# Four changes to a forward-and-backward kernel of linear and windowed attention: grouped score products, TensorE transposes, larger DMAs, an overlapped linear backward

## The chip, the cores and the metric

The kernel runs on one core of a Trainium2 chip. The metric is the device time of one execution in microseconds (us), the median of several runs. The runs of one kernel in one call lay within 0.1 to 0.7% of each other, and the changed kernel run a second time, on another occasion, was 0.4% away from the first by its ratio and 0.6% in microseconds (below). So differences of whole runs under about 20 us are not trusted here; differences inside one stage of the trace, which repeat better, are.

## The reference

The input is a sequence of 2048 rows of 640 values. Four layers follow each other: linear attention (A), windowed attention (B), A, B, with shared weights, a layer norm ahead of each and a residual around each. There are 32 heads of 20 values. The outputs are the result of the forward pass and the gradients of the input and of the four weight matrices.

```python
def A(x, wqkv, wo):                       # linear attention
    q, k, v = split(x @ wqkv)             # 32 heads of 20
    phi = lambda t: where(t > 0, t + 1, exp(t)) + 1e-6
    kv = einsum("sd,se->de", phi(k), v);  z = phi(k).sum(0)
    return (phi(q) @ kv / (phi(q) @ z + 1e-6)) @ wo

def B(x, wqkv, wo):                       # window of 256
    q, k, v = split(x @ wqkv)
    s = where(0 <= i - j < 256, q @ k.T / sqrt(20), -1e9)
    return (softmax(s) @ v) @ wo

for L in (A, B, A, B): x = x + L(layernorm(x))
# outputs: x, and the gradients of sum(x * grad_out)
```

## The kernel before

The kernel goes through the layers in 128-row tiles, in nine stages: the first linear layer; two "forward pairs" (the end of an A layer, a B layer, and the start of the next A layer, interleaved over tiles); then backwards a windowed stage, a linear stage, a windowed stage, the weight gradients of B, a linear stage, and the weight gradients of A. A scheduler orders the instructions of each engine when the program is built; each engine then runs its own list in order. "Priority" below means that the scheduler is told to place these instructions as early as it can.

A windowed backward stage works on 256 steps a layer. A step is one 128-row query tile, two heads, and up to three key tiles. It computes the scores again (`s`), their exponential (`e`, on ScalarE, masked on GpSimd), dP (`dp`), dS = dP * e (`ds`, on VectorE), the transpose of dS (`dsT`), and 18 small products that add up dV, dK and dQ (`acc`). Work on neighbouring tiles (dense products, layer norm gradient) is given out between the steps as filling. The code below is shortened.

```python
# one step: scores now; dP two steps later; the products three steps after that
for j in range(2):
    r0 = HP * (2 * p + j)                      # rows 0,32 or 64,96 of the array
    self.mm(s[:, j, 0:cw], Q["qT"][r0:r0+HP, bi, gs], K["kT"][r0:r0+HP, kk:kk+nb, gs], True, True, (r0, 0))
nc.scalar.activation(e, s, ACT.Exp)            # ... masks on GpSimd
st.q1.append(...); self.core_step(st, l)       # lag1 = 2, lag2 = 3

def core_ds(...):
    dp = st.pD.tile([P, 2, 512], F32)
    for j in range(2):
        self.mm(dp[:, j, 0:cw], Q["dT"][bi][r0:r0+HP, g, :], K["vT"][r0:r0+HP, kk:kk+nb, gs], True, True, (r0, 0))
    nc.vector.tensor_tensor(out=ds, in0=dp, in1=e, op=ALU.mult)
    self.dma(dT, ds, transpose=True)           # one DMA, or two where nb < 3
```

The linear backward is one function that runs a tile from end to end:

```python
def linear_tile(self, st, l, t, WT, g_out):
    # load dn, v, pk, pq of this tile (four DMAs); 18 transposes on TensorE
    # 21 small products -> dqkv (VectorE, ScalarE)
    self.dma(self.rows(self.dq[l], t), dqkv)   # store, 480 KB
    yield from self.tail(st, l, t, dqkv, WT, g_out)
def tail(...):                                 # load hn and g (two DMAs)
    self.dma(dT, dqkv, transpose=True)
    # 30 dense products of dT with WT, then the layer norm gradient, then a store
```

The softmax here doesn't subtract the row's maximum and nothing guards it: scores larger than these inputs give would overflow.

## Time and profile before

The kernel took 3540.01 us (median of 3 runs, 3529.01 to 3542.17).

The first view is the table of busy time by stretch of the kernel before. The stretches are the nine stages in the order named above, cut where the trace shows the first or last instruction of each. The columns are the stretch, its length, the busy time of each engine with its number of instructions (PE is TensorE, PEld its weight loads, DVE VectorE, ACT ScalarE, POOL GpSimd), the mean granted TensorE clock as a share of full speed, the mean busy share of the 16 DMA engines, and what they moved.

```profile
core 0: us, PE busy (x) PEld busy (x) DVE busy (x) ACT busy (x) POOL busy (x), PEclk, DMA share, GB/s
0.00:156.00 156.00, 101.37 (x740) 69.64 (x740) 98.33 (x291) 43.74 (x98) 17.62 (x53) 0.92 0.51 162
156.00:631.00 475.00, 380.07 (x4665) 246.50 (x4665) 265.44 (x676) 210.71 (x218) 166.96 (x274) 0.82 0.48 130
631.00:1008.00 377.00, 291.61 (x4175) 182.10 (x4175) 193.58 (x486) 178.87 (x135) 163.46 (x277) 0.81 0.59 156
1008.00:1793.00 785.00, 584.81 (x6534) 323.67 (x6534) 399.34 (x622) 274.55 (x481) 219.62 (x500) 0.60 0.75 163
1793.00:2088.00 295.00, 138.99 (x1108) 94.74 (x1109) 91.98 (x240) 45.24 (x114) 0.48 (x1) 0.69 0.47 122
2088.00:2862.00 774.00, 580.68 (x6530) 322.23 (x6529) 400.27 (x622) 274.88 (x480) 216.37 (x495) 0.60 0.70 150
2862.00:3051.00 189.00, 175.46 (x960) 94.83 (x960) 10.18 (x17) 6.21 (x13) 0.00 (x0) 0.95 0.56 177
3051.00:3347.00 296.00, 132.18 (x1105) 91.74 (x1104) 92.19 (x241) 44.64 (x112) 0.00 (x0) 0.69 0.62 166
3347.00:3536.00 189.00, 174.98 (x960) 94.56 (x960) 11.29 (x19) 6.18 (x12) 0.00 (x0) 0.96 0.37 121
```

The two windowed stages (785 and 774 us) are 44% of the span, and their TensorE clock is 0.60. The two linear stages (295 and 296 us) have TensorE busy for less than half of the time, and no other engine busier than that: something is waited for one after the other.

The next view is the same table for the scores-to-scores part of the first windowed stage, cut into its first 64 steps (two chunks) and the other 192.

```profile
1032.00:1197.00 165.00, 106.94 (x1150) 54.77 (x1150) 63.54 (x101) 53.83 (x98) 43.26 (x99) 0.53 0.55 127
1197.00:1699.00 502.00, 425.10 (x5029) 238.21 (x5028) 300.65 (x455) 209.50 (x357) 172.91 (x394) 0.61 0.82 170
```

The first 64 steps take 2.6 us each although TensorE is busy in only 65% of the time. What it waits for stands in the view of one tile, dsT, over these steps (the lines say who waited for the tile: microseconds in total, number of times):

```profile
  PEld L142: 62.4, 62
  PE acc L142: 47.7, 50
DMA to landing us min/median/max: 2.2/2.6/5.9
```

(In the second layer the first 64 steps took 183 us, but there the first scores ran ahead, beside the end of the linear stage.)

In the other 192 steps (2.61 us each) TensorE is busy in 85% of the time. How the scores and dP look there is shown by the timeline of TensorE alone (columns: start, length, engine, line, operation and tiles, sizes, number of instructions); both pairs ran at half clock:

```profile
1450.98 0.50 PE L142 MATMUL dp<-vT,dT 32*128 32x384 bf16 x2
...
1451.86 0.50 PE L142 MATMUL s<-kT,qT 32*128 32x384 bf16 x2
1452.29 1.25 PE L142 MATMUL dense<-WoTB,gT 128*128 128x320 bf16 x4
```

The pair of scores started at 1451.86 and the next work at 1452.29: a pair holds the engine for 0.43 us, and a step has two pairs.

In the linear stages the timeline of all engines shows the chain of one tile:

```profile
1912.60 0.32 SPq L117 DMA_DIRECT2D dqkv<-dqa  x1
1912.97 2.82 SPq L117 DMA_TRANSPOSE dqT<-dqa  x1
...
1918.13 5.79 PE L142 MATMUL dense<-WTA,dqT 128*128 128x320 bf16 x30 [8.59 <-DMA dqT<-dqa]
```

The bracket says that TensorE stood idle for 8.59 us until the transpose landed. Over fourteen tiles it waited 124.5 us for this tile, 8.9 us of each 17.2 us:

```profile
  PE dense L142: 124.5, 14
```

### The profile page before, as it was taken

The numbers are of one execution on the slowest core, as the hardware profiler recorded it, in microseconds if no ns is written. First come the engines' busy times: TensorE is split into PE (matmuls) and PEld (weight loads), VectorE is DVE, ScalarE is ACT, GpSimd is POOL, SyncE is SP. The second block draws the span as 40 slices with busy tenths as digits, with TensorE's granted clock in tenths as the row PEclk, the third lists the DMA queues.
The fourth block names the chain that finished last, engine by engine and source line by source line (L and its number), as shares of the span: only waits on it lengthen the run. The fifth ranks groups of instructions, "written<-read, shape, count | busy, mean of one in ns | idle before, by whom it ended". The sixth has DMA issues, their size and how long they took to land. (4 is left out here: it accounts for less than half of the span.)

```text
span 3536.7 us, 66383 instructions
## 1 busy us (share of the span) xinstructions
PE 2560.2 (72%) x26776; PEld 1520.0 (43%) x26776; DVE 1562.6 (44%) x3212; ACT 1085.0 (31%) x1661; POOL 784.5 (22%) x1600
## 2 busy tenths in 40 slices
PE   6787788688855788888544445888888669644499
PEld 4455555355522444444333322444444344333254
DVE  6555555455522566565432332555666410133200
ACT  2244444255532444444111112444444200011100
POOL 1033333245521333333100002333333100000000
PEclk9888788788865565656666665566666689866699
DMA  6455444566564888787654443888886474564542
GB/s 208 116 138 131 128 128 119 151 162 176 150 162 105 161 185 179 174 180 139 166 144 119 120 117 81 173 179 175 175 184 149 118 238 156 141 187 126 163 137 69
DMA packets 964981, 531.60 MB, mean 150 GB/s; under 512 B 686656, under 2 KB 929344, under 8 KB 964672
## 3 DMA queue, kind: packets, MB, share of 16 engines
q1 hardware_dynamic: 964672, 527.35, 60.5%
q8 instruction: 209, 3.42, 0.4%
q14 instruction: 100, 0.82, 0.1%
HBM read 216.53 MB, written 146.54 MB: 103 GB/s over the span
## 5 line engine op out<-in xcount | busy, mean ns | idle before, releaser
L626 DVE TENSOR_TENSOR ds<-dp,e 128x768 bf16<-128x768 f32 (+2 forms) x512 | 463.5, 905 | 375.3 <-PE dp L142 269.7
L595 ACT ACTIVATE e<-s 128x768 bf16<-128x768 f32 (+2 forms) x512 | 394.7, 771 | 495.4 <-PE s L142 270.7
L597 POOL TENSOR_SCALAR_AFFINE_SELECT e<-e 128x256 bf16<-128x256 bf16 x512 | 224.9, 440 | 1224.0 <-ACT e L595 1196.3
L348 ACT ACTIVATE eT<-sT 128x1536 bf16<-128x1536 f32 (+2 forms) x256 | 351.0, 1371 | 368.8 <-PE sT L142 340.3
L142 PEld LDWEIGHTS <-dqT 128*128 128x128 bf16 x1920 | 218.6, 119 | 448.1 <-DMA dqT<-dqa 285.4
L142 PE MATMUL dense<-WTA,dqT 128*128 128x320 bf16 x960 | 190.8, 375 | 281.1 <-DMA dqT<-dqa 281.1
L142 PE MATMUL s<-kT,qT 32*128 32x384 bf16 (+2 forms) x1024 | 267.1, 436 | 91.2 <-ACT e L595 87.1
L142 PE MATMUL acc<-ks,dsT 128*128 128x20 bf16 x2880 | 216.8, 179 | 134.8 <-DMA dsT<-ds 132.9
L142 PE MATMUL acc<-qs,ds 128*128 128x20 bf16 x2880 | 277.3, 179 | 13.4 <-DVE dq L680 11.9
L142 PE MATMUL dp<-vT,dT 32*128 32x384 bf16 (+2 forms) x1024 | 254.4, 441 | 39.1 <-DVE ds L626 34.3
L142 PEld LDWEIGHTS <-ds 128*128 128x128 bf16 x2880 | 212.7, 102 | 133.8 <-issue 128.5
L142 PE MATMUL acc<-ds,e 128*128 128x20 bf16 x2880 | 269.2, 177 | 0.0
L534 ACT ACTIVATE dh<-dense,rs 128x320 f32<-128x320 f32 x128 | 67.5, 527 | 652.9 <-issue 347.9
L350 POOL TENSOR_SCALAR_AFFINE_SELECT eT<-eT 128x512 bf16<-128x512 bf16 x256 | 164.6, 643 | 431.8 <-ACT eT L348 416.4
L142 PE MATMUL wg<-rq,lh 128*128 128x480 bf16 x1280 | 259.5, 366 | 0.0
L142 PEld LDWEIGHTS <-hnT 128*128 128x128 bf16 x1920 | 189.1, 106 | 130.6 <-DVE hnT L184 40.0
L142 PEld LDWEIGHTS <-dsT 128*128 128x128 bf16 x2880 | 155.6, 104 | 205.5 <-DMA dsT<-ds 183.0
L142 PE MATMUL dense<-WTB,dqT 128*128 128x320 bf16 x960 | 197.8, 367 | 29.3 <-DMA dqT<-dqkv 26.8
L142 PEld LDWEIGHTS <-e 128*128 128x128 bf16 x2880 | 211.9, 103 | 15.6 <-issue 9.9
L601 POOL TENSOR_SCALAR_AFFINE_SELECT e<-e 128x256 bf16<-128x256 bf16 x448 | 190.2, 425 | 0.0
L184 DVE COPY dnT<-flip 126x768 bf16<-126x768 bf16 x32 | 17.8, 558 | 380.8 <-PE flip L179 380.8
L142 PE MATMUL dense<-WB,hnT 128*128 128x320 bf16 x960 | 180.0, 334 | 7.0 <-DVE hnT L184 5.9
(132 smaller groups left out, 3800.2 us busy)
## 6 DMA issues: line engine op xcount, KB each, us to landing
rq<-dqkv SPq DMA_DIRECT2D x16, 1920.0 KB, 9.6
qs<-qs SPq DMA_DIRECT2D x64, 256.0 KB, 2.9
qT<-qT SPq DMA_DIRECT2D x64, 256.0 KB, 3.1
dqkv<-dq SPq DMA_DIRECT2D x32, 480.0 KB, 4.4
dqkv<-dqa SPq DMA_DIRECT2D x32, 480.0 KB, 3.4
kT<-kT SPq DMA_DIRECT2D x28, 512.0 KB, 3.9
vT<-vT SPq DMA_DIRECT2D x28, 512.0 KB, 4.1
ks<-ks SPq DMA_DIRECT2D x28, 512.0 KB, 4.4
```

Of the source, the lines that this page charges most:

```text
L142: return self.nc.tensor.matmul(out, lhsT=lhsT, rhs=rhs, start=start, stop=stop, skip_group_check=True, **kw)
L184: eng.tensor_copy(o, t[0:w, 0:n, :])
L348: nc.scalar.activation(e[:, :, 0:nb * P], s[:, :, 0:nb * P], ACT.Exp)
L350: nc.gpsimd.affine_select(out=dg, in_=dg, compare_op=ALU.is_ge, fill=0.0, base=0, pattern=[[0, 4], [1, P]], channel_multiplier=-1)
L534: nc.scalar.activation(dh[:, c * CW:(c + 1) * CW], ps[:, 0:CW], ACT.Copy, scale=rs, accum_out=ac[:, c:c + 1])
L595: nc.scalar.activation(e[:, :, 0:cw], s[:, :, 0:cw], ACT.Exp)
L597: nc.gpsimd.affine_select(out=dg, in_=dg, compare_op=ALU.is_ge, fill=0.0, base=0, pattern=[[0, 2], [-1, P]], channel_multiplier=1)
L601: nc.gpsimd.affine_select(out=fr, in_=fr, compare_op=ALU.is_ge, fill=0.0, base=-1, pattern=[[0, 2], [1, P]], channel_multiplier=-1)
L626: nc.vector.tensor_tensor(out=ds[:, :, 0:cw], in0=dp[:, :, 0:cw], in1=e[:, :, 0:cw], op=ALU.mult)
```

## The change

The change wants to keep TensorE fed in the windowed backward, relieve the DMA queue, and overlap the tiles of the linear backward.

1. **Scores and dP grouped.** Both get priority; dP is issued just ahead of the scores of a later step; the lag goes from 2 to 3, so that the dP pair and the score pair that are issued together are of different p and use opposite halves of the array. The forward scores get priority too.
2. **Half of dS on TensorE.** Steps with p = 1 transpose dS on TensorE and copy it out of PSUM (the memory that TensorE writes to) on VectorE; p = 0 still goes by DMA.
3. **Fewer, larger DMAs.** q, k and v are stored together, q and k transposed in one DMA; per-tile loads of the windowed backward become loads of two tiles, those of the linear backward of four; loads of the next slab are issued at the seventh step of a chunk, not at its start.
4. **Linear backward pipelined.** The tail of tile t-1 (its dense products) is interleaved with tile t, and the transpose is issued before the store.

The diff also gives `e` an eighth buffer, gives the linear backward a third buffer and more of PSUM, and moves one of its copies from VectorE to ScalarE.

```diff
@@ windowed core, per step
+                    if len(st.q1) >= st.lag1:
+                        self.core_dp(st, *st.q1[-st.lag1])
                     s = st.pS.tile([P, 2, 512], F32, name="s")
-                    for j in range(2):
+                    with self.tc.high_priority():
+                        for j in range(2):
                         ... the two score products ...
@@ core_ds
-        dp = ...; the two dP products
+        # moved to core_dp, with priority
         nc.vector.tensor_tensor(out=ds, in0=dp, in1=e, op=ALU.mult)
-        if nb == 3:
+        if p == 1:
+            ps = st.ps.tile([P, 8, P], BF, name="flip", tag="m")
+            for j in range(2):
+                for i in range(nb):
+                    nc.tensor.transpose(ps[:, 3 * j + i, :], ds[:, j, i * P:(i + 1) * P], self.ident)
+            nc.vector.tensor_copy(v(dT), v(ps))
+        elif nb == 3:
             self.dma(dT, ds.rearrange("p j k -> p (j k)"), transpose=True)
-            st.lag1, st.lag2 = 2, 3
+            st.lag1, st.lag2 = 3, 3
@@ backward_linear, N = 4 tiles a load
+                drive(self.linear_tile(st, l, t, L, dT), [(prev, 1.2)] if prev else [])
+                prev = back(t, L, dT)          # the tail of this tile, run beside the next
@@ linear_tile
+        self.dma(dT, dqkv, transpose=True)
         self.dma(self.rows(self.dq[l], t), dqkv)
-        yield from self.tail(st, l, t, dqkv, WT, g_out)
 ... (merged stores and loads cut)
```

More of the change, by code (lines that the diff above doesn't have):

```diff
@@ L90, in __init__ @@
         for l in (0, 2):
-            self.sv[l] = dict(pq=d(f"pq{l}", [T, D]), pk=d(f"pk{l}", [T, D]), v=d(f"v{l}", [T, DA]),
+            self.sv[l] = dict(pqk=d(f"pqk{l}", [T, 2 * D]), v=d(f"v{l}", [T, DA]),
                               dn=d(f"dn{l}", [T, DA]))
         for l in (1, 3):
-            self.sv[l] = {k: d(f"{k}{l}", [TT, P, G * P]) for k in ("qs", "ks", "vs", "qT", "kT", "vT")}
+            self.sv[l] = {k: d(f"{k}{l}", [TT, P, 3, G * P]) for k in ("s", "T")}
         self.ident = const.tile([P, P], BF, name="ident")
@@ L120, in rows, with pair @@
         return ap[t * P:(t + 1) * P, :]
+    def pair(self, ap, c, n=2):
+        return ap[c * n * P:(c + 1) * n * P, :].rearrange("(b p) f -> p b f", p=P)
     def load(self, pool, name, src, shape, dt=BF, bufs=None):
@@ L220, in a_first @@
         sv = self.sv[l]
-        f = {}
+        pqk = st.sb.tile([P, 2, D], BF, name="pqk")
         for j, nm in enumerate(("pk", "v", "pq")):
@@ L226, in a_first @@
             else:
-                pt = st.sb.tile([P, D], BF, name=nm)
+                pt = pqk[:, 0 if nm == "pq" else 1, :]
             for c in range(2):
@@ L241, in a_first @@
                 self.dma(self.rows(sv["v"], t), vt)
-                f["v"] = vt
-                yield from self.acc_outer(st, f["pk"], vt, t == 0)
-            else:
-                self.dma(self.rows(sv[nm], t), pt)
-                f[nm] = pt
+                yield from self.acc_outer(st, pqk[:, 1, :], vt, t == 0)
+        self.dma(self.rows(sv["pqk"], t), pqk.rearrange("p a f -> p (a f)"))
     def acc_outer(self, st, a, b, first):
@@ L275, in a_out @@
         nc = self.nc
-        pq = self.load(st.sb, "pqf", self.rows(self.sv[l]["pq"], t), [P, D])
+        pq = self.load(st.sb, "pqf", self.rows(self.sv[l]["pqk"], t)[:, 0:D], [P, D])
         yield
@@ L315, in b_qkv @@
         R = st.ring[t % len(st.ring)]
-        for j, nm in enumerate(("qs", "ks", "vs")):
-            s = R[nm]
+        for j, nm in enumerate("qkv"):
+            s = R["s"][:, j, :, :]
             for c in range(2):
@@ L320, in b_qkv @@
                 dst = s[:, c * HALF:(c + 1) * HALF, 0:DH]
-                if nm == "qs":
+                if nm == "q":
                     nc.vector.tensor_scalar(out=dst, in0=self.heads(ps[:, 0:CW]), scalar1=CS, scalar2=None, op0=ALU.mult)
@@ L325, in b_qkv @@
                 yield
-            flat = s.rearrange("p h d -> p (h d)")
-            self.dma(sv[nm][t], flat)
-            tn = nm[0] + "T"
-            self.dma(R[tn], flat, transpose=True)
-            self.dma(sv[tn][t], R[tn].rearrange("p g q -> p (g q)"))
-            yield
+            if j == 1:
+                self.dma(R["T"][:, 0:2, :, :].rearrange("p a g q -> p (a g) q"),
+                         R["s"][:, 0:2, :, :].rearrange("p a h d -> p (a h d)"), transpose=True)
+        self.dma(sv["s"][t], R["s"].rearrange("p a h d -> p a (h d)"))
+        self.dma(R["T"][:, 2, :, :], R["s"][:, 2, :, :].rearrange("p h d -> p (h d)"), transpose=True)
+        self.dma(sv["T"][t], R["T"].rearrange("p a g q -> p a (g q)"))
+        yield
     def b_core(self, st, l, t, o):
@@ L338, in b_core @@
         rings = [st.ring[(k0 + i) % len(st.ring)] for i in range(nb)]
-        qT = st.ring[t % len(st.ring)]["qT"]
+        qT = st.ring[t % len(st.ring)]["T"][:, 0, :, :]
         for g in range(G):
             s = st.pS.tile([P, 4, 512], F32, name="sT")
-            for i in range(nb):
-                for hh in range(4):
-                    r0 = HP * hh
-                    self.mm(s[:, hh, i * P:(i + 1) * P], rings[i]["kT"][r0:r0 + HP, g, :], qT[r0:r0 + HP, g, :],
-                            True, True, (r0, 0))
+            with self.tc.high_priority():
+                for i in range(nb):
+                    for hh in range(4):
+                        r0 = HP * hh
+                        self.mm(s[:, hh, i * P:(i + 1) * P], rings[i]["T"][r0:r0 + HP, 1, g, :], qT[r0:r0 + HP, g, :],
+                                True, True, (r0, 0))
             e = st.pe.tile([P, 4, 3 * P], BF, name="eT")
@@ L373, in b_pv @@
                 ins = self.mm(st.ops[:, 4 * q + hh, :], e[:, hh, i * P:(i + 1) * P],
-                              rings[i]["vs"][:, 4 * g + hh, 0:HA], st.first is None, i == nb - 1)
+                              rings[i]["s"][:, 2, 4 * g + hh, 0:HA], st.first is None, i == nb - 1)
                 if st.first is None:
@@ L436, in forward_pair @@
             for i in range(5):
-                R = {}
-                for nm in ("qs", "ks", "vs"):
-                    R[nm] = rp.tile([P, H, HP], BF, name=f"{nm}{i}")
-                    nc.gpsimd.memset(R[nm][:, :, DH:HP], 0.0)
-                    R[nm[0] + "T"] = rp.tile([P, G, P], BF, name=f"{nm[0]}T{i}")
-                nc.gpsimd.memset(R["vs"][:, :, DH:DH + 2], 1.0)
+                R = dict(s=rp.tile([P, 3, H, HP], BF, name=f"s{i}"), T=rp.tile([P, 3, G, P], BF, name=f"T{i}"))
+                nc.gpsimd.memset(R["s"][:, :, :, DH:HP], 0.0)
+                nc.gpsimd.memset(R["s"][:, 2, :, DH:DH + 2], 1.0)
                 st.ring.append(R)
@@ L486, in g_flip_dense, with bd @@
             yield
-    def bd(self, st, l, t, R, WoT):
+    def bd(self, st, l, t, g, o, R, WoT):
         nc = self.nc
-        g = self.load(st.sb, "gb", self.rows(self.gs[l], t), [P, D], bufs=1)
-        o = self.load(st.sb, "ob", self.rows(self.o[l], t), [P, D], bufs=1)
         ds = R["ds"]
         r = self.r[l]
-        yield
         def use(c, ps):
@@ L515, in bd, with tail @@
         yield
-    def tail(self, st, l, t, dqkv, WT, g_out):
+    def tail(self, st, l, t, dT, hn, g, gn, WT):
         nc = self.nc
-        hn = self.load(st.sb, "hnb", self.rows(self.hn[l], t), [P, D])
-        g = self.load(st.sb, "gc", self.rows(self.gs[l], t), [P, D])
-        dT = st.sb.tile([P, NF, P], BF, name="dqT")
-        self.dma(dT, dqkv, transpose=True)
-        yield
         dh = st.sf.tile([P, D], F32, name="dh")
@@ L543, in tail, with a_grad @@
         nc.vector.scalar_tensor_tensor(out=a, in0=hn, scalar=s2, in1=g, op0=ALU.mult, op1=ALU.add)
-        gn = st.sb.tile([P, D], BF, name="gn")
         nc.vector.scalar_tensor_tensor(out=gn, in0=dh, scalar=s1, in1=a, op0=ALU.add, op1=ALU.add)
-        self.dma(self.rows(g_out, t), gn)
-        st.gn = gn
         yield
-    def a_grad(self, st, l, t, g, WoT):
+    def a_grad(self, st, l, t, g, o, pq, dn, WoT):
         nc = self.nc
-        o = self.load(st.sb, "oa", self.rows(self.o[l], t), [P, D], bufs=1)
-        pq = self.load(st.sb, "pqb", self.rows(self.sv[l]["pq"], t), [P, D], bufs=1)
-        dn = st.sb.tile([P, H, HA], BF, name="dn")
         pr = st.sf.tile([P, H, DH], F32, name="prod")
@@ L569, in a_grad @@
         yield
-        flat = dn.rearrange("p h d -> p (h d)")
-        self.dma(self.rows(self.sv[l]["dn"], t), flat)
-        yield from self.acc_outer(st, pq, flat, t == 0)
+        yield from self.acc_outer(st, pq, dn.rearrange("p h d -> p (h d)"), t == 0)
     def core_chunk(self, st, l, c, half, K, Q, dq):
@@ L588, in core_chunk @@
                 for p in range(2):
+                    if len(st.q1) >= st.lag1:
+                        self.core_dp(st, *st.q1[-st.lag1])
                     s = st.pS.tile([P, 2, 512], F32, name="s")
-                    for j in range(2):
-                        r0 = HP * (2 * p + j)
-                        self.mm(s[:, j, 0:cw].rearrange("p (a b) -> p a b", a=nb), Q["qT"][r0:r0 + HP, bi, gs],
-                                K["kT"][r0:r0 + HP, kk:kk + nb, gs], True, True, (r0, 0))
+                    with self.tc.high_priority():
+                        for j in range(2):
+                            r0 = HP * (2 * p + j)
+                            self.mm(s[:, j, 0:cw].rearrange("p (a b) -> p a b", a=nb), Q["qT"][r0:r0 + HP, bi, gs],
+                                    K["kT"][r0:r0 + HP, kk:kk + nb, gs], True, True, (r0, 0))
                     e = st.pe.tile([P, 2, 3 * P], BF, name="e")
@@ L607, in core_step @@
     def core_step(self, st, l, flush=False):
+        if flush and st.q1:
+            self.core_dp(st, *st.q1[0])
         if len(st.q1) > (0 if flush else st.lag1):
@@ L616, in core_flush, with core_dp, v @@
             yield
+    def core_dp(self, st, g, gs, b, bi, p, nb, kk, cw, e, K, Q, dq, c, w0):
+        st.dp = st.pD.tile([P, 2, 512], F32, name="dp")
+        with self.tc.high_priority():
+            for j in range(2):
+                r0 = HP * (2 * p + j)
+                self.mm(st.dp[:, j, 0:cw].rearrange("p (a b) -> p a b", a=nb), Q["dT"][bi][r0:r0 + HP, g, :],
+                        K["vT"][r0:r0 + HP, kk:kk + nb, gs], True, True, (r0, 0))
     def core_ds(self, st, l, g, gs, b, bi, p, nb, kk, cw, e, K, Q, dq, c, w0):
         nc = self.nc
-        dp = st.pD.tile([P, 2, 512], F32, name="dp")
-        for j in range(2):
-            r0 = HP * (2 * p + j)
-            self.mm(dp[:, j, 0:cw].rearrange("p (a b) -> p a b", a=nb), Q["dT"][bi][r0:r0 + HP, g, :],
-                    K["vT"][r0:r0 + HP, kk:kk + nb, gs], True, True, (r0, 0))
         ds = st.pd.tile([P, 2, 3 * P], BF, name="ds")
-        nc.vector.tensor_tensor(out=ds[:, :, 0:cw], in0=dp[:, :, 0:cw], in1=e[:, :, 0:cw], op=ALU.mult)
+        nc.vector.tensor_tensor(out=ds[:, :, 0:cw], in0=st.dp[:, :, 0:cw], in1=e[:, :, 0:cw], op=ALU.mult)
         dT = st.pt.tile([P, 6, P], BF, name="dsT")
-        if nb == 3:
+        if p == 1:
+            ps = st.ps.tile([P, 8, P], BF, name="flip", tag="m")
+            for j in range(2):
+                for i in range(nb):
+                    nc.tensor.transpose(ps[:, 3 * j + i, :], ds[:, j, i * P:(i + 1) * P], self.ident)
+            def v(t):
+                return t[:, 0:6, :].rearrange("p (a b) q -> p a b q", a=2)[:, :, 0:nb, :]
+            nc.vector.tensor_copy(v(dT), v(ps))
+        elif nb == 3:
             self.dma(dT, ds.rearrange("p j k -> p (j k)"), transpose=True)
@@ L702, in backward_window @@
             st.sf = self.pool(es, "sf", 1)
+            st.sp = self.pool(es, "sp", 1)
             st.pS = self.psum(es, "pS", 1)
@@ L705, in backward_window @@
             st.pA = self.psum(es, "pA", 1)
-            st.pe = self.pool(es, "pe", 7)
+            st.pe = self.pool(es, "pe", 8)
             st.pd = self.pool(es, "pd", 5)
             st.pt = self.pool(es, "pt", 4)
-            st.lag1, st.lag2 = 2, 3
+            st.lag1, st.lag2 = 3, 3
             st.q1, st.q2 = [], []
@@ L730, in loads @@
                 Q = {}
-                for nm in ("kT", "vT", "ks"):
+                for nm, k, w in (("kT", "T", 1), ("vT", "T", 2), ("ks", "s", 1)):
                     K[nm] = sl.tile([P, 4, 4 * P], BF, name=nm)
-                    self.dma(K[nm][:, 0:n, :], sv[nm][w0:w0 + n, :, cs].rearrange("t p f -> p t f"))
-                for nm in ("qT", "qs"):
+                    self.dma(K[nm][:, 0:n, :], sv[k][w0:w0 + n, :, w, cs].rearrange("t p f -> p t f"))
+                for nm, k in (("qT", "T"), ("qs", "s")):
                     Q[nm] = sl.tile([P, 2, 4 * P], BF, name=nm)
-                    self.dma(Q[nm], sv[nm][t0:t0 + 2, :, cs].rearrange("t p f -> p t f"))
+                    self.dma(Q[nm], sv[k][t0:t0 + 2, :, 0, cs].rearrange("t p f -> p t f"))
                 for nm in ("ds", "dT"):
@@ L741, in before @@
             def before(c):
+                g = self.load(st.sp, "gb", self.pair(self.gs[l], c), [P, 2, D])
+                o = self.load(st.sp, "ob", self.pair(self.o[l], c), [P, 2, D])
+                yield
+                yield
                 for i in range(2):
                     t = 2 * c + i
-                    yield from self.bd(st, l, t, ring[t % 4], wb["WoT"])
+                    yield from self.bd(st, l, t, g[:, i, :], o[:, i, :], ring[t % 4], wb["WoT"])
             def behind(c):
+                la = l - 1
+                dT = st.sp.tile([P, NF, 2 * P], BF, name="dqT")
+                self.dma(dT, self.dq[l][2 * c * P:(2 * c + 2) * P, :], transpose=True)
+                hn = self.load(st.sp, "hnb", self.pair(self.hn[l], c), [P, 2, D])
+                g = self.load(st.sp, "gc", self.pair(self.gs[l], c), [P, 2, D])
+                yield
+                o = self.load(st.sp, "oa", self.pair(self.o[la], c), [P, 2, D])
+                pq = self.load(st.sp, "pqb", self.pair(self.sv[la]["pqk"], c)[:, :, 0:D], [P, 2, D])
+                gn = st.sp.tile([P, 2, D], BF, name="gn")
+                dn = st.sp.tile([P, 2, H, HA], BF, name="dn")
+                yield
+                yield
+                yield
                 for i in range(2):
                     t = 2 * c + i
-                    yield from self.tail(st, l, t, self.rows(self.dq[l], t), wb["WT"], g_out)
-                    yield from self.a_grad(st, l - 1, t, st.gn, wa["WoT"])
+                    yield from self.tail(st, l, t, dT[:, :, i * P:(i + 1) * P], hn[:, i, :], g[:, i, :], gn[:, i, :], wb["WT"])
+                    if i == 1:
+                        self.dma(self.pair(g_out, c), gn)
+                    yield from self.a_grad(st, la, t, gn[:, i, :], o[:, i, :], pq[:, i, :], dn[:, i, :, :], wa["WoT"])
+                self.dma(self.pair(self.sv[la]["dn"], c), dn.rearrange("p b h d -> p b (h d)"))
             for _ in before(0):
@@ L758, in core @@
                 for half in range(2):
-                    if half == 0:
-                        KQ.append(loads(c, 1))
-                    elif c + 1 < NC:
-                        KQ.append(loads(c + 1, 0))
-                    yield from self.core_chunk(st, l, c, half, *KQ.pop(0), dq)
+                    for i, _ in enumerate(self.core_chunk(st, l, c, half, *KQ.pop(0), dq)):
+                        if i == 6:
+                            if half == 0:
+                                KQ.append(loads(c, 1))
+                            elif c + 1 < NC:
+                                KQ.append(loads(c + 1, 0))
+                        yield
             for c in range(NC):
@@ L780, in backward_linear, with loads, back, linear_tile @@
         sv = self.sv[l]
+        N = 4
         with ExitStack() as es:
-            st = self.state(es, 2, 6)
-            st.sf = self.pool(es, "sf", 2)
-            wa = self.weights(es, "A", ("WT",))
-            for t in range(TT):
-                for _ in self.linear_tile(st, l, t, wa["WT"], g_out):
-                    pass
-    def linear_tile(self, st, l, t, WT, g_out):
+            st = self.state(es, 3, 8)
+            st.sf = self.pool(es, "sf", 3)
+            st.sp = self.pool(es, "sp", 2)
+            WT = self.weights(es, "A", ("WT",))["WT"]
+            def loads(c):
+                L = {}
+                for nm, src, w in (("dn", sv["dn"], DA), ("v", sv["v"], DA), ("pqk", sv["pqk"], 2 * D),
+                                   ("hn", self.hn[l], D), ("g", self.gs[l], D)):
+                    L[nm] = self.load(st.sp, "l" + nm, self.pair(src, c, N), [P, N, w])
+                L["gn"] = st.sp.tile([P, N, D], BF, name="gn4")
+                return L
+            def back(t, L, dT):
+                i = t % N
+                yield from self.tail(st, l, t, dT, L["hn"][:, i, :], L["g"][:, i, :], L["gn"][:, i, :], WT)
+                if i == N - 1:
+                    self.dma(self.pair(g_out, t // N, N), L["gn"])
+            nxt = loads(0)
+            prev = None
+            for t in range(TT):
+                if t % N == 0:
+                    L = nxt
+                if t % N == 2 and t + N < TT + 2:
+                    nxt = loads(t // N + 1)
+                dT = st.sb.tile([P, NF, P], BF, name="dqT")
+                drive(self.linear_tile(st, l, t, L, dT), [(prev, 1.2)] if prev else [])
+                prev = back(t, L, dT)
+            for _ in prev:
+                pass
+    def linear_tile(self, st, l, t, L, dT):
         nc = self.nc
-        sv = self.sv[l]
+        i4 = t % 4
         acols = [HA * h for h in HS]
@@ L794, in linear_tile @@
         dqkv = st.sb.tile([P, QT], BF, name="dqa")
-        src = {}
-        for nm, w in (("dn", DA), ("v", DA), ("pk", D), ("pq", D)):
-            src[nm] = self.load(st.sb, "l" + nm, self.rows(sv[nm], t), [P, w])
+        src = dict(dn=L["dn"][:, i4, :], v=L["v"][:, i4, :], pq=L["pqk"][:, i4, 0:D], pk=L["pqk"][:, i4, D:2 * D])
         fl = {}
-        for nm, K, cols, eng in (("dn", KA, acols, nc.vector), ("v", KA, acols, nc.scalar), ("pk", KB, kcols, nc.vector)):
+        for nm, K, cols, eng in (("dn", KA, acols, nc.vector), ("v", KA, acols, nc.scalar), ("pk", KB, kcols, nc.scalar)):
             fl[nm] = self.flip(st.ps, st.sb, src[nm], nm + "T", K, 6, 0, eng, cols)
@@ L823, in linear_tile @@
                 yield
+        self.dma(dT, dqkv, transpose=True)
         self.dma(self.rows(self.dq[l], t), dqkv)
-        yield from self.tail(st, l, t, dqkv, WT, g_out)
+        yield
     def weight_grads(self, kind, layers):
```

## The prediction

> **What bounds it now.** From first and last instructions, the 3537 us span is: first layer 150 us; forward pairs 495 and 357; windowed backward 783 and 773; linear backward 297 and 295; weight gradients 192 and 190 (untouched). The windowed backward has 512 steps. In its steady chunks (1250 to 1700 us) a step takes 2.63 us; matmul starts in the trace show about 2.08 us of TensorE work and 0.55 us of waits (scores 0.22, dP 0.13, dsT products 0.11). TensorE bounds it, at a clock near 0.62. DMA is close: the table by stretch has it 0.68 to 0.95 busy, over half in 256-byte transpose packets, and SyncE spends 227 of 450 us issuing dsT transposes (1.22 us each). In the first two chunks of a layer (69 steps, 190 us) TensorE works 111 us and waits 56 for dsT. The linear backward is a serial chain: of a 17.2 us tile TensorE waits 8.7 us for the transposed dqa (5.2 us from issue to landing).
>
> **What changes.**
> 1. Lag 3 lets dP and scores use opposite row groups. The Trainium skill (TensorE: Matmul & The Clock Gate, The mechanism) says such matmuls overlap, starting about 4 ns apart; the trace agrees inside a pair, while scores followed by dP on the same rows cost 0.27 us more. But in the built order only about a third of the steps hold all four products together: I expect 0.05 to 0.1 us a step.
> 2. Half of the dsT transposes move to TensorE: 1440 transposes of 0.107 us (clock 0.5) or 0.056 us (1.0), about 0.27 us a step, plus a 0.56 us VectorE copy per two steps (VectorE, 0.6 busy, rises to 0.7). DMA falls from 0.85 to about 0.65 busy. In steady chunks this burdens TensorE, the bound, to relieve DMA, which is not: nearly a wash (2.5 to 2.7 us). In the first two chunks most of the 56 us wait goes. With steadier loads and a paired tail: 50 us a layer.
> 3. Linear backward: the tail of tile t-1 is interleaved with tile t. But in the built order only six transposes stand between tile t's last product and the first dense product that needs its dqT, so the wait stays exposed, about 4.5 us instead of 8.7. A tile takes 13.5 to 15 us; with a slower start: 40 us a stage.
> 4. Forward: scores earlier, fewer DMAs; waits before sT are 22 us in each pair: 10 us a pair.
>
> **Sum.** 3540 - 100 - 80 - 20 = 3340 us; 8 in 10 between 3230 and 3440. Chances: faster by over 2% 0.93, within 2% 0.06, slower 0.01.
>
> **What would show it.** Item 1: starts 4 ns apart across scores and dP in a third of the steps. Item 2: dsT waits in the first chunks mostly gone, a step there about 2.2 us; a steady step near 2.6 us. Item 3: a tile near 14 us, TensorE still waiting 4 to 5 us for dqT. Item 4: pairs 1 to 4% shorter.
>
> **What would make it wrong.** The skill (same page, What's actually happening) has the clock at half or full by recent activity; the trace's clock record agrees (0.5 and 1.0 only). If denser work keeps it at 1.0 longer, steady chunks gain up to 0.4 us a step (150 us). Transposes waiting for VectorE's dS in the in-order queue, or sharing PSUM banks, could cost 0.2 us a step. Bulk loads ahead of dqT could eat item 3.

## The result, and the profile after

The changed kernel took 3312.25 us (median of 3 runs, 3311.65 to 3315.82). The ratio is 0.9367, with a 95% interval of 0.9336 to 0.9399. A ratio here is the mean time of one kernel's runs over that of the kernel before in the same rounds, so it is not quite the ratio of the medians quoted.

The table by stretch of the kernel after, for the same nine stages:

```profile
0.00:151.00 151.00, 98.00 (x744) 68.39 (x745) 98.69 (x291) 43.69 (x98) 17.05 (x43) 0.95 0.50 165
151.00:582.00 431.00, 342.90 (x4666) 232.11 (x4662) 256.07 (x677) 209.61 (x218) 165.49 (x274) 0.89 0.50 144
582.00:979.00 397.00, 292.56 (x4175) 190.64 (x4175) 191.68 (x485) 178.75 (x135) 163.26 (x267) 0.78 0.55 149
979.00:1712.00 733.00, 587.19 (x7261) 365.53 (x7262) 455.80 (x750) 275.23 (x481) 209.90 (x500) 0.67 0.58 138
1712.00:1937.00 225.00, 137.09 (x1099) 101.80 (x1098) 93.54 (x224) 55.56 (x129) 0.00 (x0) 0.74 0.50 142
1937.00:2678.00 741.00, 593.14 (x7254) 366.51 (x7254) 455.27 (x751) 275.41 (x481) 208.99 (x496) 0.67 0.57 134
2678.00:2867.00 189.00, 175.86 (x960) 95.02 (x960) 10.19 (x17) 6.35 (x13) 0.00 (x0) 0.95 0.59 183
2867.00:3108.00 241.00, 138.99 (x1106) 102.95 (x1104) 94.36 (x225) 55.26 (x128) 0.00 (x0) 0.73 0.52 148
3108.00:3309.00 201.00, 174.75 (x960) 94.36 (x960) 10.84 (x18) 6.17 (x12) 0.00 (x0) 0.94 0.56 177
```

Read against the table of before, and with the sums that the prediction made (it cuts the two forward pairs at another place, as 495 and 357 us, where the table above has 475 and 377):

| stages | predicted | measured |
|---|---|---|
| first layer and two forward pairs | -20 | -5, -44, +20: -29 |
| two windowed backward stages | -100 | -52, -33: -85 |
| two linear backward stages | -80 | -70, -55: -125 |
| two weight gradient stages | 0 | 0, +12 |
| sum | -200 | -227 |

The same cut of the first windowed stage into 64 and 192 steps:

```profile
1003.00:1127.00 124.00, 102.28 (x1211) 61.67 (x1211) 72.09 (x126) 52.36 (x96) 44.75 (x102) 0.53 0.52 136
1127.00:1607.00 480.00, 423.32 (x5611) 266.61 (x5612) 341.09 (x542) 211.05 (x357) 162.37 (x392) 0.73 0.60 137
```

The first 64 steps fell from 165 to 124 us, the other 192 from 502 to 480 although TensorE has 12% more instructions to do there; its clock went from 0.61 to 0.73, and the DMA share from 0.82 to 0.60. The waits for dsT in the first 64 steps:

```profile
  PEld L145: 12.8, 15
  PE acc L145: 9.0, 11
DMA to landing us min/median/max: 2.2/2.7/4.5
```

So 47.7 us of waiting before the products became 9.0 us; a single DMA transpose takes as long as before.

The timeline of TensorE shows what a grouped step looks like at half clock:

```profile
1302.88 0.47 PE L145 MATMUL s<-kT,qT 32*128 32x384 bf16 x1 [0.26 <-ACT e L581]
1302.89 0.50 PE L145 MATMUL dp<-vT,dT 32*128 32x384 bf16 x1
1302.89 0.50 PE L145 MATMUL s<-kT,qT 32*128 32x384 bf16 x1
1302.89 0.50 PE L145 MATMUL dp<-vT,dT 32*128 32x384 bf16 x1
1303.32 0.82 PE L623 MATMUL flip<-ident,ds 128*128 128x128 bf16 x6
```

All four products start within about 0.01 us of each other (13 ns in the trace) and hold the engine until 1303.32, for 0.44 us, the time of one pair before. The Trainium skill (TensorE: Matmul & The Clock Gate, The mechanism) has matmuls in different row groups overlap, with starts about 4 ns apart; this trace agrees.

In the linear backward:

```profile
1800.00 4.02 SPq L117 DMA_TRANSPOSE dqT<-dqa  x1
...
1804.08 0.57 SPq L117 DMA_DIRECT2D dqkv<-dqa  x1
...
1806.09 1.51 PE L145 MATMUL dense<-WTA,dqT 128*128 128x320 bf16 x5 [6.59 <-DMA dqT<-dqa]
```

The transpose now goes first and the dense products come in fives between the work of the next tile, but TensorE still stands idle for it, over thirteen tiles 67.5 us, 5.2 us a tile. The tile takes 13.6 us.

```profile
  PE dense L145: 67.5, 13
```

Two stretches got longer. In the second forward pair 377 us became 397. The view of waits there shows what TensorE waited for ahead of the forward scores (sT), the merged transpose of q and k; before the change it waited 3.3 us for the transpose of k:

```profile
PE sT L145 <- DMA T<-s: 20.7, 16, 2.4
```

And between the last scores of a windowed stage and its end, 94 and 93 us became 105 and 102. The longest single wait for DMA there, in the first layer, is for the transposed load of the gradient rows; first the kernel after, then the kernel before:

```profile
engine line waited for: us in total, times, longest us
PEld L145 <- DMA dqT<-dqkv: 14.8, 1, 14.8
PEld L142 <- DMA dqT<-dqkv: 10.3, 1, 10.3
```

In the second layer it went from 9.8 to 11.5 us. The pair of tiles is now loaded into a single buffer, but that is not what held this load: the products that last read the buffer had started by 1599.4 us, and the load was issued at 1632.9 us, when the stores of the rows that it reads (issued at 1628.7 and 1629.3 us) had landed. Most of the loss lies ahead of it: the first of these stores went out 21 and 19 us after the last scores, 14 and 13 us before the change. Why they go out later was not tried.

The last weight gradient stage starts 12 us later because four loads of its right-hand side, which the kernel before had fetched during the linear stage, are issued after that stage; this is read from the timeline and was not tried.

### The profile page after: what moved, and what is told of

Read it like the earlier page. It is cut to its first block, busy times and chain, and to the rows that moved or that the text cites. A ratio compares the mean times of both kernels' runs of the same rounds, so it can differ in the third digit from the quotient of the medians.

```text
span 3309.7 us, 67700 instructions
## 1 busy us (share of the span) xinstructions
PE 2540.5 (77%) x28216; PEld 1617.3 (49%) x28216; DVE 1666.5 (50%) x3436; ACT 1106.0 (33%) x1693; POOL 764.7 (23%) x1580
## 5 line engine op out<-in xcount | busy, mean ns | idle before, releaser
L583 POOL TENSOR_SCALAR_AFFINE_SELECT e<-e 128x256 bf16<-128x256 bf16 x512 | 213.8, 418 | 791.6 <-ACT e L581 774.2
L145 PEld LDWEIGHTS <-dqT 128*128 128x128 bf16 x1920 | 204.1, 118 | 329.1 <-DMA dqT<-dqa 168.2
L145 PE MATMUL dense<-WTA,dqT 128*128 128x320 bf16 x960 | 217.2, 375 | 163.8 <-DMA dqT<-dqa 163.8
L145 PE MATMUL s<-kT,qT 32*128 32x384 bf16 (+2 forms) x1024 | 216.4, 405 | 75.8 <-ACT e L581 67.7
L145 PE MATMUL acc<-qs,ds 128*128 128x20 bf16 x2880 | 264.4, 178 | 9.3 <-DVE dq L679 7.1
L145 PE MATMUL dense<-WTB,dqT 128*128 128x320 bf16 x960 | 210.6, 369 | 40.4 <-DMA dqT<-dqkv 38.0
L145 PE MATMUL dp<-vT,dT 32*128 32x384 bf16 (+2 forms) x1024 | 223.9, 416 | 20.8 <-DVE ds L617 19.2
L898 DVE CAST wr<-wg 128x480 bf16<-128x480 f32 (+1 forms) x36 | 21.7, 602 | 368.2 <-PE wg L145 368.2
L145 PEld LDWEIGHTS <-lh 128*128 128x128 bf16 x1280 | 125.2, 98 | 133.7
L623 PE MATMUL flip<-ident,ds 128*128 128x128 bf16 x1440 | 189.0, 273 | 0.9 <-DVE ds L617 0.9
L587 POOL TENSOR_SCALAR_AFFINE_SELECT e<-e 128x256 bf16<-128x256 bf16 x448 | 183.0, 408 | 0.0
```

The costliest lines, as they stand in the source:

```text
L145: return self.nc.tensor.matmul(out, lhsT=lhsT, rhs=rhs, start=start, stop=stop, skip_group_check=True, **kw)
L583: nc.gpsimd.affine_select(out=dg, in_=dg, compare_op=ALU.is_ge, fill=0.0, base=0, pattern=[[0, 2], [-1, P]], channel_multiplier=1)
L587: nc.gpsimd.affine_select(out=fr, in_=fr, compare_op=ALU.is_ge, fill=0.0, base=-1, pattern=[[0, 2], [1, P]], channel_multiplier=-1)
L623: nc.tensor.transpose(ps[:, 3 * j + i, :], ds[:, j, i * P:(i + 1) * P], self.ident)
L898: nc.vector.tensor_copy(r[:, 0:w], a[:, 0:w])
```

## The experiments

Each experiment edits the changed kernel. "First 64" and "other 192" are the steps of the windowed backward, in microseconds, for the two layers; the changed kernel has 124 and 121 for the first 64, and 481 and 489 for the other 192.

### The changed kernel once more

> The changed kernel itself once more, as the measure for the runs beside it: 3312 us within 10, ratio 0.937 within 0.004. If chips or rounds differ by more, the comparisons of a few tens of us between calls are not safe.

It took 3330.57 us, ratio 0.9406 (0.9381 to 0.9431), 0.0039 from the first. So the ratio is just inside the expected range and the time is 8 us outside it; runs of different calls are compared below by their ratios and by stages. The windowed steps were 126 and 120, 485 and 487; the linear stages 225 and 241; the forward pairs 438 and 397. So the linear stages repeat within 1 us, the windowed steps within 4, and the first forward pair and the first windowed stage within 7 (431 and 438, 733 and 740).

### All of dS by DMA again

```diff
-        if p == 1:
+        if p == 2:      # never
```

> The changed kernel with all of dS transposed by DMA again (lag 3 and priorities kept). Theory: the TensorE transposes pay in the first two chunks of each layer, where dsT was waited for, and are a wash later: first 64 steps of each layer 121 to 124 us back to 160 to 185, the other 192 steps within 15 us of 481 to 489, total 3390 to 3430. Rival: grouping brought the windowed gain: total within 20 us of 3312. Second rival: DMA relief brought the steady gain too: the 192 steps rise by over 20 us a layer.

It took 3390.94 us, ratio 0.957 (0.9556 to 0.9584). The first 64 steps took 162 and 158 us, the other 192 took 488 and 488. The table by stretch of this run, first layer:

```profile
1009.00:1170.00 161.00, 99.79 (x1108) 52.43 (x1105) 62.92 (x101) 53.56 (x98) 45.20 (x102) 0.51 0.58 132
1170.00:1658.00 488.00, 401.43 (x5038) 229.22 (x5039) 298.29 (x447) 208.43 (x355) 166.73 (x390) 0.64 0.85 172
```

The theory holds (158 us lies just under its range): the TensorE transposes pay 38 us a layer in the first two chunks, where dsT was waited for, and next to nothing (3 us, within the spread) later, although the DMA share there is 0.85 without them and 0.60 with them. Neither rival holds.

### All of dS on TensorE

```diff
-        if p == 1:
+        if p >= 0:      # always
```

> The changed kernel with all of dS transposed on TensorE, none by DMA. Theory: TensorE bounds the steady chunks, so another three transposes and half a VectorE copy a step cost there what half of them would cost unhidden: the last 192 steps of a layer rise from 481 to 489 us to 510 to 540; the first 64 gain little (their remaining dsT wait is 12 us): total 3350 to 3420. Rival: DMA still holds the steady chunks back (0.60 busy in the changed kernel): they fall below 475 us and the total below 3300.

It took 3407.67 us, ratio 0.9645 (0.9621 to 0.9669). The first 64 took 120 and 116 us, the other 192 took 539 and 535. The DMA share fell to 0.30 and the stage got slower by 50 us a layer. So DMA is not what holds the steady chunks, and TensorE (with VectorE, which does the copies) is. Between 1150 and 1600 us TensorE was busy for 0.92 of the time and VectorE for 0.72; no run parts the two.

### Scores and dP ungrouped

```diff
-                    if len(st.q1) >= st.lag1:
-                        self.core_dp(st, *st.q1[-st.lag1])
-                    with self.tc.high_priority():      # scores; dP likewise
-            self.core_ds(st, l, *st.q1.pop(0))
+            q = st.q1.pop(0); self.core_dp(st, *q); self.core_ds(st, l, *q)
-            st.lag1, st.lag2 = 3, 3
+            st.lag1, st.lag2 = 2, 3
```

> The changed kernel with dP issued beside dS again, lag 2, and no priority in the windowed backward; half of dS stays on TensorE. Theory: grouping is worth 0.05 to 0.1 us a step: total 3335 to 3365, nearly all in the later 192 steps of each layer. Rival: grouping is worth nothing here: within 15 us of 3312. Second rival: without it the TensorE transposes wait for dS at once and the stage is slower than before the change: over 3400.

It took 3419.27 us, ratio 0.9645 (0.9629 to 0.9661). The first 64 took 144 and 138 us, the other 192 took 527 and 526. My theory fell: grouping is worth about 42 us a layer in the steady chunks, 0.2 us a step, and 19 us in the first 64 steps. The second rival was right in size: without grouping the TensorE transposes make the steady chunks slower than they were before the change. Its reason is not seen: just ahead of these transposes TensorE waited for dS only 1.7 us in the 192 steps of the first layer. Together with the run before this gives a two-by-two of the other 192 steps (both layers):

| | all dS by DMA | half of dS on TensorE |
|---|---|---|
| not grouped | 502, 501 (kernel before) | 527, 526 |
| grouped | 488, 488 | 481, 489 (changed kernel) |

Grouping is worth 14 us a layer where dS goes by DMA, and 42 us where half of it goes by TensorE. The transposes cost 25 us a layer without grouping and nothing with it. So the two changes do not add up: each does more for the other than by itself. (The kernel before differs from the rest of the table in its loads and in one buffer as well.)

### Only the lag, only the priority

```diff
-            st.lag1, st.lag2 = 3, 3                    # run one: lag 2
+            st.lag1, st.lag2 = 2, 3
-                    with self.tc.high_priority():      # run two: no priority,
+                    if True:                           # scores and dP
```

> The changed kernel with lag 2 in the windowed backward, so dP and the scores issued beside it use the same row groups; priorities kept. Without lag 3 and priorities both, the windowed stages took 107 us more. Theory: the opposite row groups are the smaller part, because only a quarter of the steps start dP and scores together in the trace: 20 to 45 us more than 3312. Rival: row groups are the whole of it: 80 us or more. Second rival: nothing.

> The changed kernel with lag 3 kept but no priority for scores and dP in the windowed backward. Theory: the priority keeps dP, and so dS, well ahead of the transposes that wait for it in the in-order queue, and is the larger part of the 107 us: total 3370 to 3410, the steady 192 steps at 510 to 520 us a layer. Rival: the lag alone does it: within 15 us of 3312.

With lag 2 it took 3347.44 us, ratio 0.9487 (0.9458 to 0.9516): the other 192 steps 515 and 511, the first 64 at 122 and 118. Without priority it took 3400.0 us, ratio 0.9628 (0.9602 to 0.9653): the other 192 at 528 and 521, the first 64 at 140 and 134. The sizes fell about where the theories had them (528 and 521 lie just above the range), and the priority is the larger part. In the steady chunks it is nearly the whole: without it, and with lag 3 kept, they take as long as with all of the grouping undone (527 and 526). The lag is worth about 28 us a layer, but only where the priority is kept. To see how, I added up from the matmul starts how long scores and dP hold TensorE (from the first start of a cluster of them to the next other matmul, waits inside it and at its end included; the second column is these waits), in the steady chunks of the first layer:

| | us a step | of this, idle | clusters of four on opposite rows | of these, all four started together | granted clock |
|---|---|---|---|---|---|
| before | 1.05 | 0.24 | 11 in 185 steps | 7 | 0.61 |
| changed | 0.71 | 0.09 | 68 in 187 steps | 41 | 0.73 |
| lag 2 | 0.84 | 0.13 | 56 in 188 steps | 30 | 0.63 |
| no priority | 0.89 | 0.17 | 49 in 187 steps | 34 | 0.67 |
| ungrouped | 0.92 | 0.12 | 13 in 183 steps | 5 | 0.65 |
| all of dS by DMA | 1.02 | 0.29 | 59 in 192 steps | 31 | 0.64 |

Clusters of four come to 36% of the steps in the changed kernel, but only 41, about a fifth of the steps, start all four products together as in the timeline above; in the others the second pair follows later, at the median by the 0.45 us of a whole pair, and most of them overlap little or not at all. Nor does grouping alone bring the 0.71 us: with all of dS by DMA the sum is 1.02 us. There the busy part fell by 0.08 us against the kernel before (0.73 and 0.81), but the waits stayed. And the reason that I gave for the lag is not borne out: with lag 2 nearly as many steps have all four products on opposite rows, since the scheduler mixes neighbouring steps anyway. What differs more with lag 2 is the clock: a pair that stands alone holds the engine for 0.27 us at full and 0.43 us at half clock, and 107 of 202 such pairs ran at full clock in the changed kernel, 43 of 189 with lag 2. Without priority, the waits just ahead of the TensorE transposes rise from 0.0 to 13.7 us over this stretch, as the theory had it, but that is under a third of the loss of 47 us; the larger part is in the scores and dP, which hold the engine 0.18 us a step longer, about 34 us (7.5 us of the waits are counted in both).

### The priority of the forward scores

```diff
-            with self.tc.high_priority():
-                for i in range(nb): ...
+            for i in range(nb): ...
```

> The changed kernel without the priority of the forward scores, all else kept. In the changed kernel the first forward pair went from 475 to 431 us, the second from 377 to 397. Theory: the priority does both (it feeds ScalarE earlier where there is dense work to fill with, and stalls the in-order TensorE queue where there is little): pair one back to 465 to 480, pair two back to 370 to 380, total about 3330. Rival: the merged q and k transposes and stores do it: both pairs stay at 431 and 397 within 8 us, total within 10 us of 3312.

It took 3331.16 us, ratio 0.9392 (0.9374 to 0.941). The first pair took 452 us (431 and 438 with priority, 475 before), the second 382 us (397 and 397 with priority, 377 before). For the second pair the theory holds: the priority costs it 15 of the 20 us. The view of waits agrees: without the priority, TensorE waits for the merged transpose ahead of the scores for 4.0 us, not 20.7:

```profile
PE sT L145 <- DMA T<-s: 4.0, 5, 1.3
```

With the priority the scores stand earlier in TensorE's list, and the engine waits there until their operand has landed. In the first pair the same wait is longer with the priority too (16.9 us, 2.5 without), but the pair is shorter. For the first pair the theory holds by half: the priority is worth 14 to 21 us there, and the other 23 us came with the merged stores, loads and transposes, the other edits that touch that stage; they were not tried apart.

### The linear backward without interleaving

```diff
-                drive(self.linear_tile(st, l, t, L, dT), [(prev, 1.2)] if prev else [])
-                prev = back(t, L, dT)
+                drive(chain(self.linear_tile(st, l, t, L, dT), back(t, L, dT)), [])
```

> The changed kernel with the linear backward's tail run after its own tile, not beside the next one; four-tile loads and the transpose ahead of the store kept. Theory: the interleaving shortened the tile from 17.2 to 13.6 us: here 16 to 17 us a tile, total 3385 to 3420. Rival: fewer, larger DMAs did: tile stays under 14.5 us, total within 25 us of 3312.

It took 3418.6 us, ratio 0.9641 (0.9623 to 0.9659). The linear stages took 274 and 290 us, and a tile 16.5 us in its common case. The theory holds: the interleaving is worth 49 us a stage, of the 70 and 55 gained. The four-tile loads, the transpose ahead of the store and the other small edits together bring a tile from 17.2 only to about 16.5 us. The Trainium skill (DMA: Bandwidth & Descriptors, Rules for kernel authors) advises to coalesce many small transfers into one large one, since under 64 KB one pays mostly overhead; here the loads had 160 to 168 KB before they were merged, and merging them did little in this stage: TensorE still waited 100.7 us over thirteen tiles for the one transpose.

### The tail two tiles behind

```diff
-                drive(self.linear_tile(st, l, t, L, dT), [(prev, 1.2)] if prev else [])
-                prev = back(t, L, dT)
+                drive(self.linear_tile(st, l, t, L, dT), [(prev.pop(0), 1.2)] if len(prev) > 1 else [])
+                prev.append(back(t, L, dT))
```

> The changed kernel with the tail of the linear backward run two tiles behind, not one, so that the transpose has a whole tile to land. Theory: the 5 us that TensorE waits for dqT in each 13.6 us tile vanish and the tile falls to 8.5 to 10 us, bound by TensorE or DMA: total 3170 to 3230. Rival: DMA (0.5 busy) or VectorE bounds the tile already: over 12 us, total over 3280.

It took 3117.48 us, ratio 0.8838 (0.8807 to 0.8869), better than the theory expected. The linear stages took 131 and 144 us. The table by stretch of this run for the first of them (131 us over 16 tiles is 8.2 us a tile), to be read against the fifth line of the table of the kernel after:

```profile
1715.00:1846.00 131.00, 105.91 (x1093) 84.68 (x1092) 91.89 (x224) 54.49 (x128) 0.00 (x0) 0.90 0.92 242
```

TensorE now waits for dqT in five of fourteen tiles, 16.0 us in all, against 67.5 us in thirteen:

```profile
  PE dense L145: 16.0, 5
```

Its clock rose from 0.74 to 0.90, which the expectation had not counted; and DMA is busy 0.92 of the time and may be the next bound, which was not tried. This also shows that the exposed transpose was the limit of the change's pipeline, as the prediction read it from the built order.

### What the runs point to, together

```diff
-            with self.tc.high_priority():
+            with (self.tc.high_priority() if st.prio else ExitStack()):   # first pair only
-        if p == 1:
+        if p == 1 or c < 2:          # first two chunks: all of dS on TensorE
 ... and the tail two tiles behind, as above
```

> The version that the earlier runs point to: tail two tiles behind in the linear backward (3117 us by itself), priority of the forward scores in the first pair only (the second pair took 15 us less without), and all of dS on TensorE in the first two chunks of each layer (4 us a layer less there). If the parts add up: 3117 - 15 - 8 = about 3094 us, between 3080 and 3110. If they disturb each other: 3117 or more.

It took 3112.53 us, ratio 0.8779 (0.8755 to 0.8804), beside 3330.57 us for the changed kernel in the same call: 218 us faster than that, and the fastest of all by its ratio. In microseconds it missed my range by 3. By stage, against the changed kernel: the second pair took 385 us (397), the linear stages 129 and 149 (225 and 241), and the first 64 steps 122 and 116 (126 and 120), which is no more than the windowed steps differ between two runs of one kernel. Against the version with the deeper pipeline alone, only the ratio tells it apart (0.878 and 0.884, intervals just not touching). They were run at other times.

## Why the prediction was right

The total of 3312 us lies 28 us under the predicted 3340 and well inside the range. The prediction was right in its main steps; some terms were mis-sized in both directions, and that they nearly cancel is luck.

- **Steady chunks a wash for the TensorE transposes: right, but only together with the grouping.** Predicted "nearly a wash (2.5 to 2.7 us)" a step; measured 2.5 us, and 488 us without them against 481 to 489 us with them. From each start to the next matmul, the transposes of dS hold TensorE for 54.9 us in the 192 steps of the first layer, 0.29 us a step against the predicted 0.27. Without the grouping they cost 25 us a layer, a condition that the prediction did not name.
- **First two chunks: right, a little too small.** Predicted 2.2 us a step; measured 1.9. The waits for dsT went from 47.7 to 9.0 us. Of the 41 us of the first layer, undoing the transposes gives back 38.
- **Grouping, "0.05 to 0.1 us a step": right by itself, mis-sized together with the transposes.** Fewer steps than the expected "about a third" start all four products together, 41 of some 190. These are 34 more than before; at 0.43 us saved in each they make 0.08 us a step (an estimate from these counts and the time of a pair), and undoing the grouping where dS goes by DMA costs 0.07 us a step. With half of dS on TensorE it costs 0.2. I had added the two terms as if they were independent. In the traces, scores and dP hold TensorE for 1.05 us a step before, 1.02 with grouping alone, 0.92 with the transposes alone and 0.71 with both. The transposes take away most of the waits in these sums (from 0.29 to 0.09 us where the steps are grouped), and only with both does the clock reach 0.73, after 0.61, 0.64 and 0.65. The prediction named the clock as a thing that could make it wrong.
- **Clock.** The Trainium skill (TensorE: Matmul & The Clock Gate, What's actually happening) has the clock at half or full, by recent activity. The clock records here hold only 0.5 and 1.0, and the share at 1.0 rose when the gaps went. But no run set the clock by itself, so how much of the windowed gain it carries, why lag 2 loses it, and why it rises only where grouping and transposes come together, stays open.
- **Linear backward, "about 4.5 us instead of 8.7" and "a tile near 14 us": right.** Measured 5.2 us and 13.6 us. The 40 us a stage were too few (70 and 55 measured) because I took off too much for a slower start: 16 tiles at 3.6 us less are 58 us, and the first result of the stage came after 4 us (9 before) in one stage and 20 us (17 before) in the other.
- **Forward, "10 us a pair": wrong for the second pair, in sign.** The priority that feeds ScalarE earlier made it 15 us slower, with 16.7 us more of waiting for the transposed q and k ahead of the scores; the first pair gained 44. I had only looked at the waits to be saved (22 us each), not at what TensorE's list, worked in order, would do where a score's operand comes late and there is little else to run.
- **"Paired tail" as a gain: wrong, about 10 us a layer the other way.** The wait for the transposed load after the last scores grew from 10.3 to 14.8 us and from 9.8 to 11.5 us, and the stores that it needs went out later. The single buffer is not the cause of that wait, as the times above show; what is stays open.
- **Not foreseen:** the last stage started 12 us later.

So the sum was nearer than its parts, by luck: the linear backward gave 45 us more than predicted and the first pair 34 more; the second pair gave 30 less, the windowed stages 15 less, and the last stage took 12.

## What to carry to other kernels

Moving work from a busy engine that is not the bound to the one that is pays only where that work is really waited for, and where something else makes room for it: here the transposes paid in two chunks of eight and would have cost time in the others without the grouping. Two changes to one stage can also be worth more together than apart, so they should be undone one at a time and together. A software pipeline should be checked in the built order of the slow chain's consumer: if the first instruction that needs a slow transfer stands right behind its start, the pipeline is one stage too short, and one more stage was worth nearly as much here (195 us) as the whole change (228 us). Priority for the products that feed another engine helped here where there was filling work, and hurt where their operands came late and the engine waited for them in order.

## What the Trainium skill lacked or had wrong

- DMA: Bandwidth & Descriptors, DMA Transpose (X-bar): it gives constraints but no time of a transpose between SBUF tiles (SBUF is the on-chip working memory). The only time found elsewhere is for a single block of 128x128 (VectorE: DVE Perf Modes, The three transpose paths: 1309 ns). In the steady chunks before, one of 128x768 took 1.2 us of SyncE's queue and landed after 2.7 us at best, 3.4 us at the median; in the linear stage after, one of 128x1920 landed after 4.1 us at best. In the steady chunks they ran as 256-byte packets of 18 ns at the median and 25 ns in the mean, which by the mean would be 164 GB/s on 16 engines (256 B x 16 / 25 ns, an estimate), and the one issued at 1912.97 us in the linear stage before moved its 1920 packets in 2.6 us, 190 GB/s; the 261 GB/s in the page's section on latency and other measured facts was not reached by these.
- TensorE: Matmul & The Clock Gate, PE-mode transpose: the quoted duration of about 275 ns agrees (the mean record of the 1440 transposes is 273 ns), but what counts in a row of them is the distance of starts, which this section does not give: 107 ns at half and 56 ns at full clock, the same as the page has for matmuls of 128 columns.
- The same page, the same section, says that transposes do not engage the full clock. The clock in the steady chunks was 0.64 with all of dS by DMA and 0.73 with half of it transposed on TensorE, and of the dS transposes that directly followed another in the first layer 204 of 432 started at full clock. This does not show that they raise it, but they did not keep it down.
